# A delta-rule attention with a mixture-of-experts behind it: how the 64×64 triangular inverses are split between VectorE and TensorE

## The chip, the cores and the metric

The kernel runs on one core of one Trainium2 chip. The core has TensorE (matrix products into PSUM; PE in the profile, with PEld for its weight loads), VectorE (DVE), ScalarE (ACT), GpSimd (POOL) and SyncE (SP, which here only issues DMAs). The metric is the device time of one execution in microseconds. Each engine runs its instructions in the order in which they stand in its queue.

## The reference, cut to what matters

```python
# 4 batches x 8 heads, 768 positions, 40 features per head
for t in range(S):
    y[:, :, t] = einsum('bhd,bhde->bhe', rt, state)
    Sa = einsum('bhde,bhe->bhd', state, at)
    state_decay = state * wt - einsum('bhd,bhe->bhde', Sa, bt)
    state = state_decay + einsum('bhd,bhe->bhde', vt, kt)
# x = y as 3072 tokens of 320 features
logits = x @ w_gate;  P = exp(logits - max);  8 rounds of row and column normalisation of P
out = sum over 8 experts e of  P[:, e] * (relu(x @ w1[e]) @ w2[e])      # 320 -> 1024 -> 320
```

Everything is float32. The state of each head is updated 768 times one after the other; the kernel does this in chunks of 64 positions. Within a chunk the 64 updates depend on each other through a unit triangular 64×64 matrix I + L, so each chunk of each head needs its inverse T.

## The kernel before, in words

**Attention.** There are 12 chunks c of 64 positions, and 4 batches b; one pair (c, b) treats 8 heads, packed as NP = 4 pairs p of two heads h. Three kinds of work run at once:

- `prep` (lines 115–178) loads a chunk's inputs, forms decay products (scans `q` and `g` on VectorE, products `kb` and `ab` on GpSimd), multiplies `kb` and `ab` on TensorE (`ll`, line 159), and writes the triangular factor `lt` to a DRAM buffer `ld`. It fills one of NSX buffer sets (`sx`, `bb`, `cc`); a set is used again when the step that reads it has been done, so prep runs ahead of the recurrence by at most NSX pairs (c, b).
- The inversion, per group of two chunks (6 groups). `load_lu` reads the diagonal 32-blocks of 128 matrices back from `ld`, one block per partition. VectorE then inverts them: `inv_diag` the 8-blocks, `inv_8` from 8 to 16, `inv_16` from 16 to 32, with `contract` (lines 193 and 196: a broadcast product and a reduction). The result `un` and its transpose `tn` are written to DRAM (`finish`, lines 369–372).
- `tload` and `tmat` (lines 234–268) read the blocks back in a layout with the block's rows on partitions. For each of 16 heads-and-batches p and both heads of a pair, `tmat` merges two 32-blocks into a 64-block by two products on TensorE (`gp`, line 261; `op`, line 266), with ScalarE copies between (262, 263, 267, 268). The result stands as a block-diagonal 128×128 matrix `tt` for two heads. It is done in two halves of 8 p per chunk.
- `recur` runs the recurrence: per (c, b) the products `av`, `xc`, `pu` (line 308, the product with T), `c` and `zt`, each 4 matmuls, with evacuations on VectorE and ScalarE between. Four batches are interleaved (SKEW = 1.1).

The Python list `ev` gives each piece a time in units of a fifth of a chunk; the pieces are emitted in this order, and a planner that works with estimated durations then sets the order of each engine's queue. A float32 matmul of the program is two instructions of the TensorE queue, each with a weight load, so that the profile counts twice as many as the order does (a transposition, `zt` or `kt`, is one). In the last 20 us of attention the planner mixes in the first products of the second part.

**Mixture of experts.** Products `p` (line 582, a Strassen-like scheme with 7 products) and `op` (line 647, the second layer) run from about 485 us to the end, in an order that is mostly written out by hand. The change touches nothing of it. Its buffers use the memory that the attention's sets leave.

## Time and profile before

| | |
|---|---|
| time, median of 3 runs | 1840.1 us (1836.47 to 1844.41) |
| the profiled execution's own time | 1832.94 us |
| its span (first to last instruction) | 1831.2 us |
| TensorE busy over the span | 1724.3 us (94%) |
| VectorE / ScalarE / GpSimd busy | 1365.3 / 856.8 / 874.0 us |
| first and last `pu` product (line 308) | 117.4 and 500.7 us |
| first and last `op` product of the merge (line 266) | 114.3 and 489.7 us |

A busy time of TensorE counts each matmul from its start to its modelled end, so it overlaps and is not work at peak; the distance from one weight load to the next in a row of equal matmuls tells what one costs. In a row of the timeline, the columns are start and length of the piece in us, the engine, the line, the operation, out<-in, the shapes, and the number of instructions merged.

### The profile page before, as it was taken

How to read it: one execution, taken by the hardware profiler on the slowest of the kernel's cores; microseconds unless marked ns; L12 is line 12 of the kernel's file. 1: busy time of each engine (PE TensorE's matmuls, PEld its weight loads, DVE VectorE, ACT ScalarE, POOL GpSimd, SP SyncE). 2: the span in 40 equal slices, each digit the busy share in tenths (PEclk: the TensorE clock that was granted, in tenths of full speed). 3: DMA queues.
4: the chain of work that ended last, by engine and by line, in shares of the span. 5: the costliest groups of instructions: out<-in, count | busy, mean ns of one | idle time of the engine just before them, and what ended most of it. 6: DMA issues, size and time to landing. Idle time of an engine off the chain costs nothing.

```text
span 1831.2 us, 31655 instructions
## 1 busy us (share of the span) xinstructions
PE 1724.3 (94%) x11843; PEld 1696.8 (93%) x11843; DVE 1365.3 (75%) x2356; ACT 856.8 (47%) x1851; POOL 874.0 (48%) x854
## 2 busy tenths in 40 slices
PE   4479988999989999999999999999999999999999
PEld 4368888898978999999999999999999999999999
DVE  7786996973788867777676878977686877767675
ACT  6347767766743533434343434345343343424342
POOL 6545664723462626447291735008182644628160
PEclk8568988999999999999999999999999999999999
DMA  7468777867520101111020112201020111102001
GB/s 193 116 157 185 175 180 174 186 137 172 152 77 20 57 20 57 38 39 57 20 75 20 57 37 61 69 1 60 16 76 20 57 38 38 57 20 75 15 24 44
DMA packets 211759, 140.47 MB, mean 77 GB/s; under 512 B 162965, under 2 KB 193813, under 8 KB 211605
## 3 DMA queue, kind: packets, MB, share of 16 engines
q1 hardware_dynamic: 207925, 132.70, 27.9%
q10 hardware_dynamic: 3680, 5.74, 1.2%
q8 instruction: 94, 1.54, 0.3%
q14 instruction: 60, 0.49, 0.1%
HBM read 110.78 MB, written 27.61 MB: 76 GB/s over the span
## 4 chain that ended last, share of the span: by engine, by line
PE 75%; DVE 7%; DMA 4%; issue 4%; POOL 3%; ACT 2%; SPq 2%; POOLq 0%; ACTq 0%; DVEq 0%
PE op L647 36%; PE p L582 33%; DMA inp<-in_inp_dram 1%; PE xc L297 1%; PE av L289 1%; PE pu L308 1%; DVE pr L193 1%; DVE hl L606 1%; DVE q L124 1%; PE c L315 1%; DMA ld<-lt 1%; PE op L266 1%; DVE sm L600 1%; PE ll L159 1%; POOL ab L154 1%
## 5 line engine op out<-in xcount | busy, mean ns | idle before, releaser
L582 PE MATMUL p<-xch,wh 128*128 128x384 f32 (+1 forms) x1792 | 605.0, 339 | 8.9 <-DVE sm L600 4.3
L603 ACT ACTIVATE hh<-sm 128x384 fp32r<-128x384 f32 x512 | 269.5, 527 | 728.5 <-DVE sm L600 728.4
L647 PE MATMUL op<-wh,hh 128*128 128x320 f32 x1536 | 477.2, 311 | 4.0 <-ACT hh L603 3.8
L647 PE MATMUL op<-wl,hh 128*128 128x320 f32 x1536 | 474.8, 310 | 0.0
L647 PE MATMUL op<-wh,hl 128*128 128x320 f32 x1536 | 468.0, 309 | 0.9 <-DVE hl L606 0.9
L528 POOL TENSOR_TENSOR wl<-ws,wh 128x640 fp32r<-128x640 f32 x60 | 103.1, 1718 | 606.2 <-ACT wh L526 606.1
L606 DVE SCALAR_TENSOR_TENSOR hl<-sm,hh 128x384 fp32r<-128x384 f32 x512 | 373.1, 762 | 2.6 <-ACT hh L603 1.8
L582 PEld LDWEIGHTS p<-xch,wh 128*128 128x128 f32 (+1 forms) x1792 | 337.0, 188 | 13.3 <-DVE sm L600 5.2
L582 PE MATMUL p<-xcl,wh 128*128 128x384 f32 x896 | 302.3, 337 | 0.0
L582 PE MATMUL p<-xch,wl 128*128 128x384 f32 x896 | 301.8, 337 | 0.0
L647 PEld LDWEIGHTS op<-wh,hh 128*128 128x128 f32 x1536 | 290.2, 189 | 4.9 <-ACT hh L603 4.9
L647 PEld LDWEIGHTS op<-wl,hh 128*128 128x128 f32 x1536 | 291.1, 190 | 0.0
L647 PEld LDWEIGHTS op<-wh,hl 128*128 128x128 f32 x1536 | 286.8, 188 | 1.4 <-DVE hl L606 1.2
L600 DVE TENSOR_TENSOR sm<-p,u 128x384 f32<-128x384 f32 x384 | 236.3, 625 | 8.7
L582 PEld LDWEIGHTS p<-xcl,wh 128*128 128x128 f32 x896 | 168.6, 188 | 0.0
L582 PEld LDWEIGHTS p<-xch,wl 128*128 128x128 f32 x896 | 168.5, 188 | 0.0
L600 DVE TENSOR_TENSOR sm<-p,p 128x384 f32<-128x384 f32 x128 | 71.3, 557 | 129.4 <-PE p L582 75.0
L600 DVE TENSOR_TENSOR p<-p,p 128x384 f32<-128x384 f32 x128 | 71.1, 556 | 101.7 <-PE p L582 101.4
L600 DVE TENSOR_TENSOR u<-p,p 128x384 f32<-128x384 f32 x128 | 70.8, 553 | 57.1 <-PE p L582 55.9
L536 POOL TENSOR_TENSOR wl<-ss,wh 128x512 fp32r<-128x512 f32 x60 | 90.3, 1505 | 28.4 <-ACT wh L533 24.2
L159 PE MATMUL ll<-ab,kb 104*128 104x128 f32 x336 | 62.8, 344 | 40.5 <-POOL kb L147 18.5
L159 PEld LDWEIGHTS ll<-ab,kb 104*128 104x128 f32 x336 | 54.2, 244 | 45.3 <-POOL kb L147 24.8
(163 smaller groups left out, 2727.3 us busy)
## 6 DMA issues: line engine op xcount, KB each, us to landing
ws<-in_wts_dram SPq DMA_DIRECT2D x60, 832.0 KB, 4.5
inp<-in_inp_dram SPq DMA_DIRECT2D x42, 451.5 KB, 4.5
gd<-g SPq DMA_DIRECT2D x48, 113.8 KB, 2.6
gl<-gd SPq DMA_DIRECT2D x48, 113.8 KB, 2.8
vz<-in_v_dram SPq DMA_DIRECT2D x48, 112.0 KB, 3.5
xd<-y SPq DMA_DIRECT2D x24, 224.0 KB, 3.5
ld<-lt ACTq DMA_DIRECT2D x40, 128.0 KB, 2.6
rb<-in_r_dram SPq DMA_DIRECT2D x96, 48.0 KB, 3.1
```

The lines of the kernel that those rows point to most:

```text
L124: nc.vector.tensor_tensor_scan(out=qr.rearrange("r p t -> r (p t)"), data0=w65[:, 260:0:-1], data1=one65, initial=0.0, op0=ALU.mult, op1=A ...
L154: eng.tensor_tensor(out=ab[64:104, :, 64:128], in0=a_in[64:104], in1=g[64:104], op=ALU.mult)
L159: nc.tensor.matmul(ll[:, p], lhsT=kb[:, p], rhs=ab[:, p], start=True, stop=True)
L193: nc.vector.tensor_tensor(out=prv, in0=a.unsqueeze(2).broadcast_to([nu, n_c, n_r, n_k]), in1=m.unsqueeze(1).broadcast_to([nu, n_c, n_r, n_ ...
L266: nc.tensor.matmul(op[:, p], lhsT=gs[:, p], rhs=t2[:, p], start=True, stop=True)
L528: g.tensor_tensor(out=wl[:, 0:640], in0=raw[:, 256:896], in1=wh[:, 0:640], op=ALU.subtract)
L536: g.tensor_tensor(out=lv[:, 3:7], in0=so[:, :, 0], in1=hv[:, 3:7, 0], op=ALU.subtract)
L582: nc.tensor.matmul(o, lhsT=w_, rhs=x_, start=(j == 0), stop=(j == 3))
L600: eng.tensor_tensor(out=out, in0=x, in1=y, op=ALU.add)
L603: nc.scalar.activation(out=hh[:, f, h], in_=sm[f][:, h], func=AF.Relu)
L606: v.scalar_tensor_tensor(out=hl[:, f, h], in0=sm[f][:, h], scalar=0.0, in1=hh[:, f, h], op0=ALU.max, op1=ALU.subtract)
L647: nc.tensor.matmul(ops[i], lhsT=a[:, h, cs], rhs=w_[:, cw], start=(f == 0 and h == 0 and j == 0), stop=(last and h == 1 and j == 2))
```

## The change

VectorE now stops at blocks of 16: `inv_16`, and the copies of the off-diagonal 16-blocks that it needed (line 201 in `flip_l`, line 369 in `finish`), are taken out for all groups. TensorE does the rest. Let D be the inverse of the diagonal 16-blocks, Dᵀ its transpose, and O the part of L outside them. `tload` now loads three 64-wide tiles per chunk: `ob` (O), `dt` (Dᵀ) and `tt` (D), each with one head on partitions 0–63 and the other on 64–127. `tmat` makes four products, each of 8 p × 2 heads with 64×64 operands: `gp` = O and Dᵀ, copied to `mt`; `op` = `mt` and D, added to D in `tt`; `gq` = `mt` and the new `tt`, copied to `mq`; `oq` = `mt` and `mq`, added to `tt`. With M nilpotent of order 4 on 16-blocks, (I + M)(I + M²)D is the inverse. The copies are on ScalarE and the additions on VectorE, each over the whole 128×512 tile.

T is now stored compactly (64 columns instead of a block-diagonal 128), and `pu` is made of 8 matmuls with 64 rows instead of 4 with 128.

`ob`, `dt` and `tt` have two buffers each (`td` and `lg` had one), `tload` is emitted 1.5 units earlier relative to `tmat`, and `tmat` one unit earlier. From the third chunk on, GpSimd clears the unused quadrants of `tt`, since the sum has filled them. There are 22 buffer sets for `prep` instead of 23.

```diff
-    tt_b = [const.tile([128, 4 * NP, 128], F32, name=f"tt{i}") for i in range(NTB)]
-    td_b = [const.tile([128, 4 * NP, 32], F32, name="td")]
-    lg_b = [const.tile([128, 4 * NP, 64], F32, name="lg")]
+    tt_b, ob_b, dt_b = ([const.tile([128, 4 * NP, 64], F32, name=f"{x}{i}") for i in range(NTB)]
+                        for x in ("tt", "ob", "dt"))
+    mt_b = const.tile([128, 4 * NP, 64], F32, name="mt")
+    mq = const.tile([128, 2 * NP, 64], F32, name="mq")
...
     def flip_l(us):
...
-        nc.vector.tensor_copy(out=lu[us, 16:32, 0:16], in_=lu[us, 0:16, 16:32].rearrange("u k r -> u r k"))
...
-    def inv_16(us, i):
-        g, un_, tn_, l16 = gt(us, 16), un[us], tn[us], lu[us, 16:32, 0:16]
...
-    INV += [(inv_8, (0,)), (inv_8, (1,)), (flip_h, ()), (inv_16, (0,)), (inv_16, (1,)), (inv_16, (2,))]
+    INV += [(inv_8, (0,)), (inv_8, (1,)), (flip_h, ())]
 
     def tload(c):
...
+        w = 16
+        if c >= NTB:
+            for h in range(0, 128, 64):
+                nc.gpsimd.memset(tt[h:h + 32, :, 32:64], 0.0)
         for h in range(2):
-            nc.sync.dma_start(out=lb[q[h], :, q[h]],
-                              in_=ld[cc, 0:32].rearrange("j b p h s -> j (b p) h s")[:, :, h, 32:64])
-        for h in range(2):
-            nc.sync.dma_start(out=t1[q[h]], in_=nd[u[0][h]].rearrange("g j s -> j g s"))
-        for h in range(2):
-            nc.sync.dma_start(out=t2[q[h]], in_=ud[u[1][h]].rearrange("g j s -> j g s"))
+            for a in range(0, 64 - w, w):
+                nc.sync.dma_start(out=ob[h * 64 + a:h * 64 + a + w, :, a + w:64],
+                                  in_=ld[cc, a:a + w].rearrange("j b p h s -> j (b p) h s")[:, :, h, a + w:64])
+        for blk in range(2):
+            for h in range(2):
+                q, r = slice(blk * 32, blk * 32 + 32), slice(h * 64 + blk * 32, h * 64 + blk * 32 + 32)
+                nc.sync.dma_start(out=dt[r, :, q], in_=nd[u[blk][h]].rearrange("g j s -> j g s"))
         for h in range(2):
             for blk in range(2):
-                r = slice(h * 64 + blk * 32, h * 64 + blk * 32 + 32)
-                nc.sync.dma_start(out=tt[r, :, r], in_=ud[u[blk][h]].rearrange("g j s -> j g s"))
+                q, r = slice(blk * 32, blk * 32 + 32), slice(h * 64 + blk * 32, h * 64 + blk * 32 + 32)
+                nc.sync.dma_start(out=tt[r, :, q], in_=ud[u[blk][h]].rearrange("g j s -> j g s"))
 
+    def tprod(name, lhs, rhs):
+        o = pt.tile([128, 2 * NP, 64], F32, name=name, tag="pt")
+        for p in range(2 * NP):
+            for h in range(0, 128, 64):
+                nc.tensor.matmul(o[h:h + 64, p], lhsT=lhs[h:h + 64, p], rhs=rhs[h:h + 64, p], start=True, stop=True)
+        return o
+
     def tmat(c, half):
         gl = slice(half * 8, half * 8 + 8)
...
-        gp = pt.tile([64, 2 * NP, 32], F32, name="gp", tag="pt")
-        for p in range(2 * NP):
-            nc.tensor.matmul(gp[:, p], lhsT=lb[:, p], rhs=t1[:, p], start=True, stop=True)
-        nc.scalar.copy(out=gs[0:32, :, 0:32], in_=gp[0:32])
-        nc.scalar.copy(out=gs[32:64, :, 32:64], in_=gp[32:64])
-        op = pt.tile([64, 2 * NP, 32], F32, name="op", tag="pt")
-        for p in range(2 * NP):
-            nc.tensor.matmul(op[:, p], lhsT=gs[:, p], rhs=t2[:, p], start=True, stop=True)
-        nc.scalar.copy(out=tt[0:32, :, 32:64], in_=op[0:32])
-        nc.scalar.copy(out=tt[64:96, :, 96:128], in_=op[32:64])
+        ob, dt, tt = (x[:, gl] for x in tts[c])
+        mt = mt_b[:, gl]
+        gp = tprod("gp", ob, dt)
+        nc.scalar.copy(out=mt, in_=gp)
+        op = tprod("op", mt, tt)
+        nc.vector.tensor_tensor(out=tt, in0=op, in1=tt, op=ALU.add)
+        gp = tprod("gq", mt, tt)
+        nc.scalar.copy(out=mq, in_=gp)
+        op = tprod("oq", mt, mq)
+        nc.vector.tensor_tensor(out=tt, in0=op, in1=tt, op=ALU.add)
...
         for p in range(NP):
-            nc.tensor.matmul(pu[:, p], lhsT=tts[c][:, b * NP + p], rhs=x1[:, p], start=True, stop=True)
+            for h in range(0, 128, 64):
+                nc.tensor.matmul(pu[h:h + 64, p], lhsT=tts[c][2][h:h + 64, b * NP + p], rhs=x1[h:h + 64, p],
+                                 start=True, stop=True)
...
-        nc.vector.tensor_copy(out=tn[us, 16:32, 0:16], in_=un[us, 0:16, 16:32].rearrange("u c j -> u j c"))
...
-        t = 5 * c + 2 - T_LEAD
+        t = 5 * c + 2 - T_LEAD - 1
...
-NSX = 23
+NSX = 22
...
-L_LEAD = 0.5
+L_LEAD = 2
```

The planner moves the work of the queues around these products. On TensorE, at the place where the first chunk's T is made and the first step of the recurrence takes it (`ll` and `kt` are products of `prep`, `xc` and `av` of the recurrence), there stood before:

```order
L167 MATMUL kt<-cst,kb 128x104 x4
L261 MATMUL gp<-td,lg 64x32 x8
L266 MATMUL op<-td,lg 64x32 x8
L261 MATMUL gp<-td,lg 64x32 x8
L308 MATMUL pu<-x_966,tt_217 128x104 x4
L297 MATMUL xc_1030<-f,sx_214 104x104 x4
```

and now:

```order
L250 MATMUL gp<-dt_215,ob_213 64x64 x15
L161 MATMUL ll<-ab_219,kb 128x128 x4
L169 MATMUL kt<-cst,kb 128x104 x4
L250 MATMUL gp<-dt_215,ob_213 64x64
L250 MATMUL op<-tt_211,mt 64x64 x16
L161 MATMUL ll<-ab_220,kb 128x128 x4
L169 MATMUL kt<-cst,kb 128x104 x4
L250 MATMUL gq<-tt_211,mt 64x64 x16
L161 MATMUL ll<-ab_219,kb 128x128 x4
L169 MATMUL kt<-cst,kb 128x104 x4
L250 MATMUL oq<-mq,mt 64x64 x16
L250 MATMUL gp<-dt_215,ob_213 64x64 x16
```

(then `ll` once, and `pu` of the first step). Between the four products stand those of three more pairs of `prep`, which before came after the first `pu`; there are 17 pairs of `ll` and `kt` ahead of the first `pu` instead of 14. The products of 64×64 form 72 separate runs in TensorE's queue before and 130 after, `pu` counted with them after.

On VectorE, after the copy that follows the 16-blocks of the first group, there stood before:

```order
L207 COPY tn<-un 128x2x8x8
L193 TENSOR_TENSOR pr<-un,lu 128x1024
L128 RECIPROCAL g_223<-q 112x4
L169 TENSOR_TENSOR st_188<-ll,cst 64x8x64
L196 TENSOR_REDUCE gt<-pr 128x8x8
L134 SCALAR_TENSOR_TENSOR g<-inp,g_223 112x260
L193 TENSOR_TENSOR pr<-un,lu 128x1024
```

and so on to the twelfth piece of `inv_16`, and now:

```order
L208 COPY tn<-un 128x2x8x8
L130 RECIPROCAL g_221<-q 112x4
L136 SCALAR_TENSOR_TENSOR g<-inp,g_221 112x260
L171 TENSOR_TENSOR st_179<-ll,cst 64x8x64
L126 SCALAR_TENSOR_TENSOR q<-inp,cst 112x260
```

What is left there is work of `prep`.

On TensorE, where the first products of the experts (`p`) stand among those of the recurrence, there stood before, with three steps (`pu`) of the recurrence still to come:

```order
L261 MATMUL gp<-td,lg 64x32
L582 MATMUL p_5735<-xch_5628,wh_5630 128x384
L582 MATMUL p_5735<-xcl_5629,wh_5630 128x384
L289 MATMUL av<-rb_231,vz_225 104x128 x4
L582 MATMUL p_5735<-xch_5628,wl_5631 128x384
```

and now, with eight steps still to come:

```order
L250 MATMUL gq<-tt_211,mt 64x64 x16
L333 MATMUL zt<-cst,z 40x104 x4
L313 MATMUL c_6338<-pm,bb_185 104x104 x4
L579 MATMUL p_7109<-xch_7002,wh_7004 128x384
L579 MATMUL p_7109<-xcl_7003,wh_7004 128x384
L579 MATMUL p_7109<-xch_7002,wl_7005 128x384
```

Eight of these products stand there together, and the next ones only after six more steps of the recurrence.

More of the change, by code (lines that the diff above doesn't have):

```diff
@@ L73, in attention @@
     luf = inv.tile([128, 1056], F32, name="lu")
-    prf = inv.tile([128, 1024], F32, name="pr")
-    gtf = inv.tile([128, 256], F32, name="gt")
+    prf = inv.tile([128, 512], F32, name="pr")
+    gtf = inv.tile([128, 64], F32, name="gt")
     tnf = inv.tile([128, 1056], F32, name="tn")
@@ L90, in clear @@
         nc.gpsimd.memset(tnf, 0.0)
-        for t in vz_b + rb_b + c1_b + lg_b:
+        for t in vz_b + rb_b + c1_b:
             nc.vector.memset(t, 0.0)
@@ L94, in clear @@
             nc.gpsimd.memset(t[96:RL], 0.0)
-        for t in tt_b:
-            nc.gpsimd.memset(t, 0.0)
+        for ts in zip(dt_b, ob_b, tt_b):
+            for t in ts:
+                nc.gpsimd.memset(t, 0.0)
     fresh = set(range(NSX))
@@ L104, in first_use @@
                            in_=cst[64:R2, 360:400].unsqueeze(1).broadcast_to([40, 8, 40]))
-    state = {"sx": 0, "ab": 0, "g1": 0, "vz": 0, "c1": 0, "t1": 0, "tt": 0, "rb": 0, "y": 0}
+    state = {"sx": 0, "ab": 0, "g1": 0, "vz": 0, "c1": 0, "t1": 0, "tt": 0, "ob": 0, "dt": 0, "rb": 0, "y": 0}
     def rot(key, lst):
@@ L238, in tload @@
         cc = GRP[c][1]
-        q = [slice(h * 32, h * 32 + 32) for h in range(2)]
         u = [[slice(cc * 64 + blk * 32 + h * 16, cc * 64 + blk * 32 + h * 16 + 16) for h in range(2)]
              for blk in range(2)]
+        w = 16
+        if c >= NTB:
+            for h in range(0, 128, 64):
+                nc.gpsimd.memset(tt[h:h + 32, :, 32:64], 0.0)
         for h in range(2):
-            nc.sync.dma_start(out=lb[q[h], :, q[h]],
-                              in_=ld[cc, 0:32].rearrange("j b p h s -> j (b p) h s")[:, :, h, 32:64])
```

17 lines of the change are left out of this document (2 added, 15 removed).

## The prediction

> **What bounds the kernel now.** I read the busy times by stretch first, then the rows of the stretch that the change touches. Columns: stretch, length, busy time and count of PE, PEld, DVE, ACT, POOL, then PE's granted clock, DMA share and GB/s.
>
> ```profile
> 0.00:117.00 117.00, 57.92 (x294) 51.55 (x294) 86.73 (x157) 56.32 (x140) 68.04 (x98) 0.63 0.66 159
> 117.00:500.00 383.00, 353.29 (x3337) 338.50 (x3337) 285.03 (x495) 264.76 (x656) 194.64 (x229) 0.93 0.75 170
> 500.00:600.00 100.00, 88.05 (x522) 83.16 (x521) 84.01 (x161) 40.37 (x79) 41.47 (x38) 0.97 0.14 44
> 600.00:1831.00 1231.00, 1225.02 (x7697) 1223.59 (x7695) 909.56 (x1545) 495.33 (x976) 569.81 (x491) 1.00 0.13 43
> ```
>
> From 600 us the experts keep TensorE full, and the change does not touch them. It acts in two stages. Up to 117 us TensorE is half idle: the first T is not there. From 117 to 500 us, the 48 steps of the recurrence, TensorE is busy 92% at a mean clock of 0.93, VectorE 74%. So work taken from VectorE there buys little by itself, and work given to TensorE costs nearly its full length. The chain that ended last says the same of the whole:
>
> ```profile
> PE 75%; DVE 7%; DMA 4%; issue 4%; POOL 3%; ACT 2%; SPq 2%; POOLq 0%; ACTq 0%; DVEq 0%
> ```
>
> **Change, part 1: what leaves VectorE.** The 128x1024 products and their sums are `inv_16`'s alone; with the last copy in `finish` (min/median/max ns):
>
> ```profile
> L193 DVE TENSOR_TENSOR pr<-gt,tn 128x1024 f32<-128x1024 f32 x18 | 22.6, 1257 | 0.0
> L193 DVE TENSOR_TENSOR pr<-un,lu 128x1024 f32<-128x1024 f32 x18 | 22.1, 1229 | 0.0
> L196 DVE TENSOR_REDUCE gt<-pr 128x64 f32<-128x1024 f32 x12 | 14.5, 1205 | 0.1
> L196 DVE TENSOR_REDUCE un<-pr 128x64 f32<-128x1024 f32 x12 | 14.4, 1203 | 0.0
> L196 DVE TENSOR_REDUCE gt<-pr 128x128 f32<-128x1024 f32 x6 | 7.2, 1204 | 0.0
> L196 DVE TENSOR_REDUCE un<-pr 128x128 f32<-128x1024 f32 x6 | 7.2, 1202 | 0.0
> L369 DVE COPY tn<-un x6: 348/369/567, 101.0 to 417.2; 128x256 f32<-128x256 f32 x6
> L290 DVE TENSOR_TENSOR f<-av,cst 104x512 f32<-104x512 f32 x48 | 32.6, 680 | 29.1 <-PE av L289 28.9
> ```
>
> That is 88.0 + 2.3 us, and as much again for the copy in `flip_l`: 92 us. Back come 48 additions of 128x512 from PSUM, nearest to the `f` row: 48 × 0.68 = 33. VectorE gains 60 us, most of it before 417 us. ScalarE's 96 copies of 0.36 become 48 of about 0.6: no change that counts.
>
> **Part 2: what TensorE gets.** The price of a matmul instruction is the distance of weight loads in a row of them. At full clock:
>
> ```profile
> L261 PEld LDWEIGHTS gp<-td,lg x384: 129/135/228, 110.4 to 484.0; 64*64 64x64 f32 x192
> L308 PEld LDWEIGHTS pu<-x,tt x384: 186/192/337, 117.4 to 500.7; 128*128 128x128 f32 x192
> L297 PEld LDWEIGHTS xc<-f,sx x512: 166/172/297, 19.4 to 496.8; 104*104 104x104 f32 x171
> 357.98 1.00 PEld L261 LDWEIGHTS gp<-td,lg 64*64 64x64 f32 x16 [1.76 <-issue]
> 355.02 0.97 PEld L308 LDWEIGHTS pu<-x,tt 128*128 128x128 f32 x8
> 360.29 1.54 PEld L297 LDWEIGHTS xc<-f,sx 104*104 104x104 f32 x16
> ```
>
> A 64x64 instruction costs (1.00 − 0.135)/15 = 58 ns, one of `pu` (0.97 − 0.192)/7 = 111 ns, one of `xc` (104 columns stream) (1.54 − 0.172)/15 = 91 ns. Before, TensorE gives 768 × 0.058 = 44.5 us to the merge and 384 × 0.111 = 42.6 to `pu`. After, it has 24 halves × 4 products × 16 matmuls × 2 = 3072 instructions in the merges and 768 in `pu`, alternating in pairs between the upper and the lower partitions. All hangs on whether two such halves overlap. The trace has one place where the last `op` (partitions 64–127) met the first `gp` (0–63), at half clock:
>
> ```profile
> 114.25 1.46 PEld L266 LDWEIGHTS op<-td,lg 64*64 64x64 f32 x13 [2.08 <-ACT lg L263]
> 115.56 0.18 PEld L261 LDWEIGHTS gp<-td,lg 64*64 64x64 f32 x1
> 115.60 0.22 PEld L266 LDWEIGHTS op<-td,lg 64*64 64x64 f32 x1
> 115.62 0.22 PEld L261 LDWEIGHTS gp<-td,lg 64*64 64x64 f32 x1
> 115.70 0.22 PEld L266 LDWEIGHTS op<-td,lg 64*64 64x64 f32 x1
> 115.73 0.22 PEld L261 LDWEIGHTS gp<-td,lg 64*64 64x64 f32 x1
> 115.81 0.22 PEld L266 LDWEIGHTS op<-td,lg 64*64 64x64 f32 x1
> ```
>
> Alone, `op` loads come every (1.46 − 0.22)/12 = 0.10 us; in the mixed stretch still every 0.10 to 0.11, and a `gp` load sits in each gap. Two for the price of one. I take this for full clock too: 29 ns per 64x64 instruction, 3072 × 0.029 = 89 us; for `pu`, whose streamed side is `xc`'s, 91/2: 768 × 0.0455 = 35. The bounds are this and no overlap (58 and 91 ns).
>
> A third term is the change of form. A row of 64x64 products between full ones:
>
> ```profile
> 347.53 0.30 PEld L308 LDWEIGHTS pu<-x,tt 128*128 128x128 f32 x2
> 347.94 1.00 PEld L266 LDWEIGHTS op<-td,lg 64*64 64x64 f32 x16
> 348.98 0.30 PEld L308 LDWEIGHTS pu<-x,tt 128*128 128x128 f32 x2
> ```
>
> The second `pu` load began at 347.64, so the next was due at 347.75 and came at 347.94; the last `op` load began at 348.81, the next was due at 348.87 and came at 348.98. In and out cost 0.19 + 0.11 = 0.30 us. The order has 72 such runs before, 130 after: 22 us against 39.
>
> Sum: before 44.5 + 42.6 + 22 = 109; after 89 + 35 + 39 = 163. TensorE gets 54 us more, and at the stage's clock of 0.93, 58 us.
>
> **Part 3: the front.** The first T came when group 0's inversion had gone through DRAM:
>
> ```profile
> 77.36 1.22 DVE L193 TENSOR_TENSOR pr<-un,lu 128x1024 f32<-128x1024 f32 x1
> 101.04 0.57 DVE L369 COPY tn<-un 128x256 f32<-128x256 f32 x1
> 106.92 2.06 PE L159 MATMUL ll<-ab,kb 104*128 104x128 f32 x8 [1.40 <-POOL kb L147]
> 110.40 1.91 PE L261 MATMUL gp<-td,lg 64*64 64x32 f32 x16 [0.73 <-DMA td<-nd]
> 117.41 2.03 PE L308 MATMUL pu<-x,tt 128*128 128x104 f32 x8
> PE ll L159 <- POOL kb L147: 17.7, 6, 4.7
> 359.03 0.97 PEld L159 LDWEIGHTS ll<-ab,kb 104*128 104x128 f32 x8
> 359.91 0.43 PEld L167 LDWEIGHTS kt<-cst,kb 104*128 104x128 f32 x4
> ```
>
> Twelve pieces of 1.2 us leave this chain: 14.6 us, so `gp` could start near 95. But the merge is longer (four products of 1.7 us at half clock and four evacuations of 0.6 to 0.7, about 11 us for the first half, against 7), and `ll` of the fourteenth pair, at 106.9, stands ahead of `gp`, with three more pairs between the four products. These come at GpSimd's pace, 6 to 7 us apart here, perhaps 4.5 without `inv_16` between their scans. So the first `pu` stays near 117 (112 to 122). What is won is that three pairs of `prep` are done by then: 3 × (0.97 + 0.43) = 4 us less for TensorE later.
>
> **Part 4: waits given back.** From 117 to 500 us TensorE is idle 29.7 us, from 500 to 600 us 12. With VectorE 60 us lighter I give back a third of the first, 10 us; four dependent products with an evacuation behind each bring new waits, so not more. Before 600 us the experts' products stand earlier among the recurrence's, but only eight of them: half of the 12, 6 us.
>
> **DMA.** Each chunk issues 14 loads instead of 10, 48 more in all, each about half a microsecond of SP:
>
> ```profile
> 108.83 2.08 SPq L252 DMA_DIRECT2D tt<-ud x4
> ```
>
> 25 us more on SP. The loads of O can go before the inversion is done, the others are emitted 2.5 units ahead of where they were, with a second buffer: I price it at nothing. What is queued behind them are `inp`, `gl`, `rb`; if these become late, see the rivals. One set less lets `prep` run ahead one pair less; nothing in the waits shows a set being late. GpSimd's 20 small clears of `tt` fall on an engine that is half idle there.
>
> Total: 58 − 4 − 10 − 6 = +38 on the profiled execution's 1832.9 us: 1871. The median of the runs lies 7 us higher, the sum stands halfway between the two: **1874 us**.
>
> **Rivals.** *The halves don't overlap at full clock.* No row shows more than two loads and two multiplications begun in 107 ns (the mixed stretch). I read this as the array at half clock; it could be the rate at which TensorE takes instructions. Then a pair costs 107 ns at any clock: 3840 × 0.0535 = 205, with 39 for the runs 244 instead of 163, +87 in all: 1961. It decides from about 45 ns per instruction. For it: the mixed stretch is cold, and the only one; against: the same clock halves the single rate as well.
>
> The Trainium skill (TensorE: Matmul & The Clock Gate, section "Wait — 56ns, not 53.3ns?") says that starts of matmuls never come closer than about 25 ns. Counted for multiplications alone this would leave the first sum standing; an estimate that counts weight loads too gives 100 ns for a pair, this rival.
>
> *VectorE's release decides: faster.* If the waits were mostly VectorE's lateness, TensorE would get back all its idle time (29.7 + 12), a clock of 1.0 instead of 0.93 (27 us of the 383), and 10 us at the front. That is 79, against 54 + 0: 1808 as the end; with two thirds of it, 1834. For it: in 0 to 117 us the clock is 0.63, which shows what idling costs, and VectorE ran 85% from 200 to 300 us:
>
> ```profile
> 200.00:300.00 100.00, 90.75 (x871) 86.93 (x869) 85.16 (x141) 71.87 (x183) 61.43 (x68) 0.93 0.81 180
> 400.00:500.00 100.00, 95.85 (x932) 92.31 (x933) 55.43 (x97) 68.22 (x160) 38.98 (x46) 0.95 0.68 163
> ```
>
> Against: from 400 to 500 us, with hardly any inversion left, TensorE is no less full. It decides when more than 54 us come back.
>
> *SP or the chain of four products paces the steps.* Half of SP's added 25 us exposed, or 0.5 us of wait at each of the 96 products with nothing of part 4 given back: some +25, 1899.
>
> **Numbers.** Forecast 0.45 (own range 1850 to 1900), no overlap 0.24, VectorE's release 0.21, pacing 0.10. What a measurement of this kernel can tell from no change is about 0.5%, 9 us: faster 0.21, same 0.10, slower 0.69. The range, 1826 to 1962, takes in the better half of the second and nearly all of the first and fourth cases.
>
> **What would show it.** Right: merge loads 29 ns apart on average at full clock; TensorE above 92% in the stage of the steps, its end 30 to 45 us later; VectorE near 65%. Wrong: loads 50 to 58 ns apart (no overlap), or steps at 8 us each as now, (500 − 117)/48, with VectorE idle (release). A first `pu` before 110 us would refute part 3.

## The result, and the profile after

| | before | after |
|---|---|---|
| time, median of 4 runs | 1838.7 us (1836.5 to 1844.4) | 1907.3 us (1905.2 to 1909.1) |
| the profiled execution's own time | 1832.9 us | 1906.5 us |
| its span | 1831.2 us | 1904.6 us |
| mean granted clock of TensorE | 0.959 | 0.957 |
| first and last `pu` product | 117.4 and 500.7 us | 113.0 and 573.3 us |

The changed kernel is slower: the ratio is 1.038, with a 95% interval of 1.036 to 1.040. That is 69 us more, where the forecast was some 35 more. The page of the kernel after, its busy times and the shares of the chain that ended last:

```profile
PE 1786.7 (94%) x14531; PEld 1741.7 (91%) x14531; DVE 1307.4 (69%) x2319; ACT 848.7 (45%) x1802; POOL 842.3 (44%) x877
...
PE 78%; DVE 7%; DMA 7%; issue 3%; SPq 2%; POOL 2%; ACT 1%; ACTq 0%; DVEq 0%; POOLq 0%
```

VectorE has lost 58 us of its 1365.3, TensorE has gained 62, and the share of DMA in the chain has gone from 4% to 7%. Where the time lies is read from the busy times by stretch, cut at each kernel's own first and last `pu` (columns as in the prediction). First the kernel before, then the kernel after:

```profile
0.00:117.40 117.40, 58.33 (x296) 51.89 (x296) 87.11 (x158) 56.32 (x140) 68.04 (x98) 0.63 0.66 159
117.40:500.70 383.30, 353.59 (x3340) 338.87 (x3339) 285.16 (x496) 264.76 (x656) 194.91 (x229) 0.93 0.75 169
500.70:1831.20 1330.50, 1312.36 (x8211) 1306.05 (x8209) 993.08 (x1704) 535.70 (x1055) 611.01 (x527) 1.00 0.13 43
```

```profile
0.00:113.00 113.00, 60.85 (x398) 54.12 (x398) 67.76 (x136) 53.95 (x133) 63.16 (x102) 0.65 0.70 171
113.00:573.30 460.30, 410.94 (x5924) 378.42 (x5925) 250.28 (x481) 259.04 (x614) 168.74 (x248) 0.93 0.61 142
573.30:1904.60 1331.30, 1314.88 (x8214) 1309.19 (x8209) 989.39 (x1704) 535.72 (x1055) 610.38 (x527) 0.99 0.13 43
```

The 73 us of span are split in this way: the front is 4.4 us shorter, the stage of the 48 steps is 77.0 longer (460.3 against 383.3), and what follows is 0.8 longer. Of the 77.0, TensorE's busy time takes 57.4 (410.9 − 353.6) and its idle time 19.6 (49.4 − 29.7). The first of these is what the prediction asked for (58). The second has the opposite sign of what it asked for (−10).

### The profile page after: what moved, and what is told of

The parts are those of the page before. It is cut to its first block, busy times and chain, and to the rows that moved or that the text cites. A ratio compares the mean times of both kernels' runs of the same rounds, so it can differ in the third digit from the quotient of the medians.

```text
span 1904.6 us, 37021 instructions
## 1 busy us (share of the span) xinstructions
PE 1786.7 (94%) x14531; PEld 1741.7 (91%) x14531; DVE 1307.4 (69%) x2319; ACT 848.7 (45%) x1802; POOL 842.3 (44%) x877
## 4 chain that ended last, share of the span: by engine, by line
PE 78%; DVE 7%; DMA 7%; issue 3%; SPq 2%; POOL 2%; ACT 1%; ACTq 0%; DVEq 0%; POOLq 0%
PE op L644 35%; PE p L579 32%; DMA inp<-in_inp_dram 3%; PE xc L293 2%; PE c L313 1%; DMA rb<-in_r_dram 1%; PE av L285 1%; PE pu L305 1%; DMA ld<-lt 1%; DVE q L126 1%; PE gp L250 1%; PE ll L161 1%; PE op L250 1%; PE gq L250 1%; PE oq L250 1%
## 5 line engine op out<-in xcount | busy, mean ns | idle before, releaser
L533 POOL TENSOR_TENSOR wl<-ss,wh 128x512 fp32r<-128x512 f32 x60 | 91.0, 1517 | 32.5 <-ACT wh L530 28.2
L708 DVE SCALAR_TENSOR_TENSOR acc<-op,pmat,acc 128x320 f32<-128x320 f32 x168 | 91.2, 543 | 4.6 <-PE op L644 4.5
L126 DVE TENSOR_TENSOR_SCAN q<-inp,cst 112x260 f32<-112x260 f32 x42 | 29.3, 698 | 92.7 <-DMA inp<-in_inp_dram 72.4
```

The source lines that it names most:

```text
L126: nc.vector.tensor_tensor_scan(out=qr.rearrange("r p t -> r (p t)"), data0=w65[:, 260:0:-1], data1=one65, initial=0.0, op0=ALU.mult, op1=A ...
L533: g.tensor_tensor(out=lv[:, 3:7], in0=so[:, :, 0], in1=hv[:, 3:7, 0], op=ALU.subtract)
L708: nc.vector.scalar_tensor_tensor(out=acc[:, m], in0=ops[i], scalar=pmat[:, n, e:e + 1], in1=acc[:, m], op0=ALU.mult, op1=ALU.add)
```

## Do the two halves overlap?

The price of the added products hung on this. A stretch of the timeline of the kernel after, TensorE's weight loads at full clock (1.00 granted from 402 to 408 us):

```profile
403.21 0.92 PEld L285 LDWEIGHTS av<-rb,vz 104*104 104x104 f32 x8
404.27 1.01 PEld L250 LDWEIGHTS gq<-tt,mt 64*64 64x64 f32 x32
405.35 0.30 PEld L333 LDWEIGHTS zt<-cst,z 104*40 104x40 f32 x4
405.63 0.81 PEld L313 LDWEIGHTS c<-pm,bb 128*104 128x104 f32 x8
406.55 0.73 PEld L305 LDWEIGHTS pu<-x,tt 64*64 64x64 f32 x16
407.41 0.44 PEld L293 LDWEIGHTS xc<-f,sx 104*104 104x104 f32 x4
L250 PEld LDWEIGHTS gq<-tt,mt x768: 129/135/228, 96.8 to 558.9; 64*64 64x64 f32 x192
L305 PEld LDWEIGHTS pu<-x,tt x768: 129/133/228, 113.0 to 573.3; 64*64 64x64 f32 x192
```

A run of 32 takes (1.01 − 0.135)/31 = 28.2 ns per instruction: two instructions of 64×64 in the time of one (58). `pu` takes (0.73 − 0.133)/15 = 39.8 ns; 45.5 had been priced. The halves overlap at full clock, and the rival "no overlap" is out. These are means: in the run of `gq`, the loads of the two halves begin 7 ns apart, and the next pair about 50 ns later.

The price of a change of form is in the same rows. A load of `av` takes about 0.18 us, so its last one begins at 403.95 and `gq` 0.32 us later; the last load of `gq` begins at 405.15 and `zt` 0.20 later. With 0.11 and 0.03 us as the usual distances, going in costs 0.21 and coming out 0.17. That is about 0.4 us for a run, and the same for `pu` between `c` and `xc` (0.30 was priced). The trace has 130 runs, as the order has. Since 28.2 and 39.8 lie under the priced 29 and 45.5, the sum comes out a little higher only: 87 + 31 + 130 × 0.4 = 170 against 163.

## Where the idle time shows: late loads

In the kernel after, `inp`, the input of `prep`, comes late more often. These are the waits of the stage for it, before and after (waiting engine and line, what it waited for, us in total, times, longest):

```profile
DVE q L124 <- DMA inp<-in_inp_dram: 17.5, 9, 5.6
```

```profile
DVE q L126 <- DMA inp<-in_inp_dram: 56.0, 13, 8.8
```

One such wait as the timeline of the kernel after shows it, SP's queue (SPq) with it:

```profile
296.60 2.25 SPq L235 DMA_DIRECT2D ob<-ld  x3
298.89 0.60 SPq L240 DMA_DIRECT2D dt<-nd  x1
...
303.11 1.65 SPq L240 DMA_DIRECT2D dt<-nd  x3
304.80 0.57 SPq L269 DMA_DIRECT2D vz<-in_v_dram  x1
305.47 0.74 SPq L120 DMA_DIRECT2D inp<-in_inp_dram  x1
306.25 0.57 SPq L269 DMA_DIRECT2D vz<-in_v_dram  x1
306.93 0.56 SPq L120 DMA_DIRECT2D inp<-in_inp_dram  x1
...
310.88 0.70 DVE L126 TENSOR_TENSOR_SCAN q<-inp,cst 112x260 f32<-112x260 f32 x1 [8.81 <-DMA inp<-in_inp_dram]
311.55 0.58 DVE L308 TENSOR_TENSOR pm<-pu,cst 128x416 f32<-128x416 f32 x1
...
312.28 0.85 PE L333 MATMUL zt<-cst,z 104*40 104x104 f32 x4 [6.68 <-DVE g L130]
```

Three loads of `dt`, 1.65 us of SP, stand ahead of `inp`, and four more loads of T, 2.85 us, a little before them. VectorE sits 8.8 us in front of the scan `q`. Behind the scan in its queue stands `pm`, which belongs to the recurrence and has nothing to do with `inp`. TensorE stands still for 6.7 us before `zt`, until VectorE's `g`, which follows the scan. So a late load for `prep` stops a step. Whether the load is late because of what stands ahead of it is what the experiment with the loads on another queue asks.

The stage has two halves: the one while `prep` still runs (up to the last `ll`), and the rest. Before, with 28 steps begun in the first and 20 in the second:

```profile
117.40:367.90 250.50, 225.81 (x2088) 216.61 (x2088) 206.37 (x352) 176.81 (x446) 149.67 (x174) 0.91 0.78 176
367.90:500.70 132.80, 127.79 (x1254) 122.25 (x1252) 78.79 (x144) 87.95 (x210) 45.24 (x55) 0.96 0.67 156
```

After, with 26 and 22:

```profile
113.00:399.30 286.30, 249.94 (x3466) 229.79 (x3467) 162.38 (x326) 169.45 (x411) 118.17 (x181) 0.92 0.68 157
399.30:573.30 174.00, 161.00 (x2461) 148.63 (x2460) 87.89 (x156) 89.59 (x203) 50.57 (x67) 0.94 0.50 117
```

TensorE's idle time goes from 24.7 to 36.4 us in the first half and from 5.0 to 13.0 in the second. A step takes 8.9 us and then 11.0 in the first half, 6.6 and then 7.9 in the second.

## Experiments

For each kernel the median is set against the median of the kernel before on the same chip, so "+55" is 55 us over that. The changed kernel stands at +69. Stage means first to last `pu`. The rows are of one execution each. The planner orders the queues anew for each kernel, so a run shows its edit together with what the new order moved.

### 1. VectorE's release alone

The kernel before, without `inv_16` and its two copies. This leaves the off-diagonal 16-blocks out of T, so part of the work is not done by anybody.

```diff
-        nc.vector.tensor_copy(out=lu[us, 16:32, 0:16], in_=lu[us, 0:16, 16:32].rearrange("u k r -> u r k"))
-    INV += [(inv_8, (0,)), (inv_8, (1,)), (flip_h, ()), (inv_16, (0,)), (inv_16, (1,)), (inv_16, (2,))]
+    INV += [(inv_8, (0,)), (inv_8, (1,)), (flip_h, ())]
-        nc.vector.tensor_copy(out=tn[us, 16:32, 0:16], in_=un[us, 0:16, 16:32].rearrange("u c j -> u j c"))
```

> The kernel before with the 16-to-32 step of the inversion left out (inv_16 and the two copies that serve it), so T lacks the off-diagonal 16-blocks; the merge on TensorE, the loads and the 23 sets stay. It gives VectorE's release alone. Theory 1 (the steps are paced by TensorE's own queue): TensorE's 353.6 busy us in the stage of the steps stay, only part of its 29.7 idle us and some of the front come back: 10 to 25 us less than before. Theory 2 (VectorE's lateness paces the steps): the stage gets shorter by about the 92 us taken out or a good part of it: 50 us less or more.

Measured: 1833.6 us, ratio 0.997 (0.995 to 0.999), −5 us. The stage of this kernel:

```profile
99.90:493.20 393.30, 359.72 (x3360) 342.47 (x3360) 219.92 (x448) 269.45 (x668) 169.25 (x235) 0.93 0.74 169
```

VectorE has 65 us less to do there than before (219.9 against 285.2), and the first `pu` comes 17.5 us earlier. The stage is nonetheless 10 us longer, and TensorE idles 33.6 us in it instead of 29.7. Part of this is work that moved: 16 pairs of `prep` have their `ll` ahead of the first `pu`, 18 in the kernel before, so two more fall into the stage. What the change takes off VectorE was worth 5 us; neither theory had it so small. The rival "VectorE's release decides" is out by the direct measurement.

### 2. The overlap taken away

The kernel after, with all products of the upper partitions first and then those of the lower ones:

```diff
-        for p in range(2 * NP):
-            for h in range(0, 128, 64):
+        for h in range(0, 128, 64):
+            for p in range(2 * NP):
```

> The changed kernel with the two loops in each merge product swapped: all 8 products of the upper partitions, then all 8 of the lower, so that neighbours in the queue are on the same half and hardly overlap. Theory 1: 3072 instructions go from 28 ns to nearly 58 ns apiece, with some overlap where the two rows of 16 meet: 60 to 90 us more than the changed kernel. Theory of late loads and chain waits as the pace (TensorE's own length does not matter any more): under 25 us more.

Measured: 1947.6 us, ratio 1.059 (1.055 to 1.063), +109, so 40 more than the changed kernel. Its stage, and a run of the merge at full clock:

```profile
107.90:614.80 506.90, 488.90 (x5940) 458.26 (x5939) 254.92 (x490) 260.79 (x617) 171.86 (x250) 0.92 0.57 131
456.31 1.76 PEld L250 LDWEIGHTS oq<-mq,mt 64*64 64x64 f32 x32
```

(1.76 − 0.135)/31 = 52.4 ns per instruction. The mean takes in the few loads in the middle where the two halves meet and overlap; the others are 58 to 59 ns apart. So without neighbours of the other half, the overlap is gone. TensorE's busy time grows by 78 us against the changed kernel, as 3072 × 24 ns = 74 ask. The time grows by only 40, because the idle time falls from 49.4 to 18.0 and the first `pu` comes 5 us earlier. With more to do, TensorE has less to wait for. Both expectations missed: 60 to 90 us, if TensorE's length set the time, was too much, and under 25, if it did not matter, too little. A little more than half of the added length was paid.

### 3. Only two of the four products

The kernel after without `gq`, `oq`, the copy to `mq` and the second addition. T then lacks the terms of second and third order in M.

```diff
-        gp = tprod("gq", mt, tt)
-        nc.scalar.copy(out=mq, in_=gp)
-        op = tprod("oq", mt, mq)
-        nc.vector.tensor_tensor(out=tt, in0=op, in1=tt, op=ALU.add)
```

> The changed kernel without its third and fourth product (gq, oq, their copy and addition left out), so T lacks the terms of second and third order. Theory 1 (TensorE's length in the stage sets the time): 1536 instructions x 28.3 ns = 43 us less, the number of runs of 64x64 products stays (126 against 130), and some waits go with the shorter chain: 43 to 60 us less than the changed kernel. Theory of late loads as the pace: the loads are all still there, so under 20 us less.

Measured: 1855.3 us, ratio 1.010 (1.006 to 1.014), +20, so 49 less than the changed kernel, within the 43 to 60 that TensorE's length asked for. The stage gives 37 of it (423.1 against 460.3) and the front 15, where the first `pu` comes at 97.8 us instead of 113.0. In its stage TensorE is busy 35 us less than in the changed kernel's. The whole stage, then its part after the last `ll`:

```profile
97.80:520.90 423.10, 375.48 (x4477) 341.73 (x4474) 241.76 (x478) 251.00 (x601) 182.88 (x257) 0.92 0.69 158
364.60:520.90 156.30, 143.47 (x1816) 130.47 (x1816) 76.00 (x148) 84.17 (x193) 50.13 (x67) 0.95 0.60 134
```

With two products the merge's instructions cost 1536 × 28.2 ns = 43 us, no more than the 44.5 of the kernel before; those of `pu` cost 31 instead of 42.6, and VectorE has no `inv_16`. Still the kernel is 1% slower than the one before. It has 126 runs of the narrow form instead of 72. At the prices read above that is 126 × 0.4 = 50 us instead of 22, which takes more than the 13 that merge and `pu` save; this part is worked out and not measured alone. TensorE's idle time in the stage is 47.6 us, nearly that of the changed kernel, and 12.8 in the second half, where the changed kernel has 13.0. So most of the excess of idle time doesn't need the chain of four products: it is there with two.

### 4. T's loads taken off SP

The kernel after, with all 14 loads of `tload` issued by ScalarE:

```diff
-                nc.sync.dma_start(out=ob[h * 64 + a:h * 64 + a + w, :, a + w:64],
+                nc.scalar.dma_start(out=ob[h * 64 + a:h * 64 + a + w, :, a + w:64],
...
-                nc.sync.dma_start(out=dt[r, :, q], in_=nd[u[blk][h]].rearrange("g j s -> j g s"))
+                nc.scalar.dma_start(out=dt[r, :, q], in_=nd[u[blk][h]].rearrange("g j s -> j g s"))
...
-                nc.sync.dma_start(out=tt[r, :, q], in_=ud[u[blk][h]].rearrange("g j s -> j g s"))
+                nc.scalar.dma_start(out=tt[r, :, q], in_=ud[u[blk][h]].rearrange("g j s -> j g s"))
```

> The changed kernel with the 14 loads of T per chunk issued from ScalarE's queue instead of SP's. Theory A (the input loads of prep come late because SP issues the many loads of T ahead of them, and block VectorE and GpSimd): VectorE's wait for inp shrinks from 72 us to under 30 and the time falls by 5 to 15 us. Theory B (SP's queue is not what makes inp late): the time stays within 5 us or grows by what ScalarE loses to 168 issues of about 0.5 us.

Measured: 1893.6 us, ratio 1.029 (1.027 to 1.031), +55, so 14 less than the changed kernel; the intervals are apart. The halves of its stage (26 and 22 steps), and the wait for `inp`:

```profile
120.20:384.50 264.30, 239.91 (x3439) 220.63 (x3440) 152.94 (x304) 164.53 (x398) 113.58 (x173) 0.95 0.72 165
384.50:558.40 173.90, 162.41 (x2463) 150.08 (x2463) 86.43 (x158) 89.28 (x203) 49.97 (x67) 0.94 0.50 117
DVE q L126 <- DMA inp<-in_inp_dram: 41.0, 11, 5.9
```

The stage is 22 us shorter than the changed kernel's, all of it in the first half, with as many steps (264.3 against 286.3); the second half is the same to 0.1. Of the 22, 12 are idle time: 24.4 us in the first half, what it was before the change. The other 10 are busy time at a higher granted clock, with the same work (239.9 × 0.95 and 249.9 × 0.92, 228 and 230 us at full clock). The waits for `inp` fall from 56 to 41 us, over the whole kernel from 72 to 51, where theory A expected under 30: the time came out as it expected, the wait only in part. The first `pu` comes 7 us later than in the changed kernel, which takes a third of the gain away; 19.5 pairs of `prep` are begun by then instead of 17.25, so a part of the stage's work has moved ahead of it. In this kernel, having the loads on SP costs 14 us in all, where they were priced at nothing.

The Trainium skill (DMA: Bandwidth & Descriptors, section "Issuing engines are not separate DMA queues") says that issuing from several engines only saves the sequencer's time, which is usually small beside the transfer. For single loads the trace agrees: SP takes 1.65 us for three loads of `dt`, and an `inp` lands 4.6 us after its issue in the median. Over the 168 loads of `tload` it was not small in this run, 14 us; experiments 5 and 7, with the same edit in other kernels, have 6 and 3 us.

### 5. The same edit on the kernel before

All ten loads of `tload` by ScalarE in the kernel before:

```diff
-            nc.sync.dma_start(out=lb[q[h], :, q[h]],
+            nc.scalar.dma_start(out=lb[q[h], :, q[h]],
...
-                nc.sync.dma_start(out=tt[r, :, r], in_=ud[u[blk][h]].rearrange("g j s -> j g s"))
+                nc.scalar.dma_start(out=tt[r, :, r], in_=ud[u[blk][h]].rearrange("g j s -> j g s"))
```

> The kernel before with the 10 loads of T per chunk issued from ScalarE's queue. Tells whether the 14 us that the same edit gave the changed kernel belong to its larger and earlier loads. If late loads behind SP are a cost of the changed kernel alone: within 5 us of the kernel before. If they are a cost of both: 8 to 14 us less.

Measured: 1829.9 us, ratio 0.996 (0.993 to 0.999), −6, between the two expectations. The stage is 1.5 us shorter, and its waits for `inp` fall from 17.5 us:

```profile
117.10:498.90 381.80, 360.81 (x3345) 342.95 (x3344) 289.18 (x500) 266.62 (x661) 193.82 (x228) 0.92 0.75 170
DVE q L124 <- DMA inp<-in_inp_dram: 10.0, 8, 3.1
```

Before the change the loads on SP cost less than half as much time. But TensorE's idle time in the stage falls here too, from 29.7 to 21.0 us, against 49.4 to 35.9 in experiment 4. Of the idle time that goes with loads on SP, the greater part was there before the change. With the loads on ScalarE in both kernels, the change costs 61 us (+55 against −6) instead of 69. By the intervals of the three ratios, what SP adds to the cost of the change lies between about 1 and 15 us. This kernel is also a little faster than both, the one before and the one after.

### 6. GpSimd's product taken out of the recurrence

Of TensorE's waits in the stage of the kernel after, those before `zt` are the largest group: four, 18.2 us together. One is the 6.7 us shown above; another ended with GpSimd's `z` (a row of its timeline):

```profile
441.23 0.88 PE L333 MATMUL zt<-cst,z 104*40 104x104 f32 x4 [5.51 <-POOL z L328]
```

The kernel after, with `z` of all chunks on VectorE (in both kernels this is so from the tenth chunk on):

```diff
-        (nc.vector if c >= 9 else nc.gpsimd).tensor_tensor(out=z, in0=ws[:, :, 64:104],
+        nc.vector.tensor_tensor(out=z, in0=ws[:, :, 64:104],
```

> The changed kernel with z of all chunks on VectorE (before: GpSimd for chunks 0 to 8). Theory A (the new idle time of TensorE comes from z standing behind work of GpSimd that waits for late loads): the idle time before zt, 18 us, loses the share in which GpSimd released it, 5 to 11 us less. Theory B (it comes from the chain of four dependent products): no change within 4 us. Theory C (z is late because pm on VectorE is late): no change or a few us more, since VectorE gets 0.33 us per step more.

Measured: 1902.8 us, ratio 1.035 (1.033 to 1.037), +64. Set against 1.036 to 1.040 for the changed kernel, this is hardly to be told from no change. The idle time before `zt` fell from 18.2 to 5.1 us, that before `gq` rose from 5.2 to 16.3. Most of what was taken away at one place came up at another.

### 7. Both edits together

The kernel after with the edits of experiments 4 and 6.

```diff
-                nc.sync.dma_start(out=ob[h * 64 + a:h * 64 + a + w, :, a + w:64],
+                nc.scalar.dma_start(out=ob[h * 64 + a:h * 64 + a + w, :, a + w:64],
...
-        (nc.vector if c >= 9 else nc.gpsimd).tensor_tensor(out=z, in0=ws[:, :, 64:104],
+        nc.vector.tensor_tensor(out=z, in0=ws[:, :, 64:104],
```

> The changed kernel with both edits that took waits away: the loads of T from ScalarE's queue, and z on VectorE. If the waits behind late loads are what they have in common and they add up: 14 + 4, so about 1889 us; TensorE's idle time in the stage falls from 49 to about 30 us, that of the kernel before, and what is left over it is TensorE's longer work, 57 us. If they remove the same wait: 1893 us as with the loads alone.

Measured: 1901.0 us, ratio 1.037 (1.034 to 1.040), +66. A miss for both expectations: the 14 us of experiment 4 are all but gone again. The stage of this kernel, then its first half:

```profile
121.10:570.30 449.20, 410.63 (x5899) 378.65 (x5899) 251.98 (x495) 253.20 (x601) 148.91 (x204) 0.93 0.62 142
121.10:391.70 270.60, 245.21 (x3439) 226.09 (x3440) 163.69 (x329) 164.18 (x398) 102.90 (x148) 0.93 0.71 161
```

The idle time is 38.6 us, 11 less than in the changed kernel, and 25.4 in the first half, so this part of experiment 4 is there again. But the granted clock is 0.93 as in the changed kernel, not 0.95, so the busy time is the changed kernel's, and the first `pu` comes 8 us later. What 4 shows firmly is the idle time in the first half, 12 us; its lower busy time hung on a clock that was not there with the other edit. Gains of this size don't add up.

### 8. `pu` in halves on the kernel before

The kernel before, `pu` made of eight products of 64 rows that take the diagonal blocks of `tt`:

```diff
-            nc.tensor.matmul(pu[:, p], lhsT=tts[c][:, b * NP + p], rhs=x1[:, p], start=True, stop=True)
+            for h in range(0, 128, 64):
+                nc.tensor.matmul(pu[h:h + 64, p], lhsT=tts[c][h:h + 64, b * NP + p, h:h + 64], rhs=x1[h:h + 64, p],
+                                 start=True, stop=True)
```

> The kernel before with pu alone changed to 8 matmuls of 64 rows (each head's 64x64 block of T). TensorE: 384 x 0.111 = 42.6 us become 768 x 0.040 = 30.5, but the order has 107 separate runs of 64x64 products instead of 72, 35 x 0.33 = 11.6 us. Theory 1: the two cancel, within 5 us of the kernel before. If changes of form cost nothing in the end: 10 us less. If the halves of pu do not overlap: 768 x 0.09 = 69, 35 us more.

Measured: 1839.1 us, ratio 1.003 (1.000 to 1.005). The halves save 384 × 111 − 768 × 39.8 ns = 12 us of `pu` and pay about 0.4 us for each of 35 more runs of the narrow form (107 in the trace instead of 72), 14. The two nearly cancel, as expected; the result, some 4 us more, is hardly to be told from nothing.

### 9. The overlap on the kernel before

The kernel before, with `op` of the first half of a chunk alternating with `gp` of the second, so that a chunk has three steps instead of four and the middle one overlaps:

```diff
+            if op is not None:
+                nc.tensor.matmul(op[:, p], lhsT=gs0[:, p], rhs=t2[:, p], start=True, stop=True)
+            if gp is not None:
+                nc.tensor.matmul(gp[:, p], lhsT=lb[:, p], rhs=t1[:, p], start=True, stop=True)
...
-        for half in range(2):
-            ev.append((t + 2 * SKEW * half, tmat, (c, half)))
+        for k in range(3):
+            ev.append((t + SKEW * k, tmat, (c, k)))
```

> The kernel before with the op products of the first half of a chunk (partitions 64 to 127) set alternately with the gp products of the second half (0 to 63). Inversion, loads and sets are unchanged. Theory 1: 12 chunks x 16 instructions x 0.058 = 11 us of TensorE's time overlap, 5 more runs cost 1.6: 5 to 12 us less than before. If TensorE's length did not set the time, within 4 us.

Measured: 1845.6 us, ratio 1.005 (1.003 to 1.007), +10, where 5 to 12 us less, or a change within 4, was expected. Its stage:

```profile
114.90:513.00 398.10, 362.65 (x3336) 345.56 (x3337) 282.95 (x495) 264.78 (x656) 194.72 (x229) 0.88 0.73 163
```

Busy time by the granted clock, as an estimate, gives 362.65 × 0.88 = 319 us of work at full clock, against 353.59 × 0.93 = 329 before. So some 10 us of work are saved. But the granted clock is lower, the idle time is 35.5 us instead of 29.7, and the stage is longer. Taking work from TensorE did not shorten it.

### 10. The merge in full form

The question was now whether TensorE's work bounds the stage at all when it is made less. The kernel before, with the merge as block-diagonal 128×128 products for two p at a time, one run of `gp` and one of `op` for a chunk, in the same form as everything around them. Half of its 16 loads are on ScalarE, and it has 22 sets:

```diff
-    lg_b = [const.tile([128, 4 * NP, 64], F32, name="lg")]
+    lg_b = [const.tile([128, 2 * NP, 128], F32, name=x) for x in ("lb", "gs")]
...
-        gp = pt.tile([64, 2 * NP, 32], F32, name="gp", tag="pt")
+        gp = pt.tile([128, 2 * NP, 32], F32, name="gp", tag="pt")
...
-            nc.tensor.matmul(gp[:, p], lhsT=lb[:, p], rhs=t1[:, p], start=True, stop=True)
+            nc.tensor.matmul(gp[:, p], lhsT=lb[:, p], rhs=t1_t[:, p], start=True, stop=True)
...
-        for half in range(2):
-            ev.append((t + 2 * SKEW * half, tmat, (c, half)))
+        ev.append((t, tmat, (c,)))
```

> The kernel before with its merge in the full 128x128 form: two p (one on partitions 0 to 63, one on 64 to 127) in one block-diagonal product, the whole chunk at once, 8 matmuls for gp and 8 for op; 8 of its 16 loads per chunk go from ScalarE's queue, and 22 sets make room. TensorE: 384 instructions x 0.111 = 43 us instead of 768 x 0.058 = 44.5, and none of the 72 changes of form (22 us). Theory 1 with the price of the form right: 15 to 25 us less than before, with 5 of it perhaps from the loads on ScalarE. If changes of form cost nothing in the end (other waits take their place): within 6 us of the kernel before.

Measured: 1856.9 us, ratio 1.012 (1.010 to 1.014), +21, a miss in sign. The halves of its stage (27 and 21 steps):

```profile
122.70:374.10 251.40, 211.77 (x1832) 205.81 (x1833) 201.94 (x336) 174.04 (x437) 142.32 (x167) 0.91 0.75 173
374.10:507.90 133.80, 122.97 (x1115) 121.33 (x1113) 80.85 (x137) 85.94 (x209) 37.96 (x47) 0.92 0.63 144
```

TensorE's busy time falls by 18.9 us (334.7 against 353.6), near what was worked out (1.5 and 22 at full clock), and its idle time rises by 20.7. The first half is as long as before the change (251.4 against 250.5) with 14 us less busy time in it. The edit does more than take work away: it has 16 loads for a chunk instead of 10, and it merges a chunk at once, so that its first step waits for all of it. This run doesn't tell these apart from the form.

### 11. One set less

The kernel before with 22 buffer sets, as the changed kernel has:

```diff
-NSX = 23
+NSX = 22
```

> The kernel before with 22 sets for prep instead of 23, nothing else. Theory (sets are not short): within 5 us of the kernel before. If one set less makes prep late: 10 us or more added, and a part of what the changed kernel lost.

Measured: 1831.8 us, ratio 0.998 (0.997 to 1.000). The missing set costs nothing in the kernel before, so it is an unlikely cause of the change's result and of that of experiment 10. (23 sets in the changed kernel were not tried.)

### 12. Both engines relieved at once

Experiment 10 with the omission of experiment 1 (T again lacks the off-diagonal 16-blocks). If TensorE and VectorE bound the stage together, taking from both should pay where taking from one does not.

```diff
-    INV += [(inv_8, (0,)), (inv_8, (1,)), (flip_h, ()), (inv_16, (0,)), (inv_16, (1,)), (inv_16, (2,))]
+    INV += [(inv_8, (0,)), (inv_8, (1,)), (flip_h, ())]
```

> The run e9 (merge in the full form, without changes of form) with the 16-to-32 step left out as in e1 (T lacks the off-diagonal 16-blocks). Each edit alone left the stage of the steps as long as it was, 385 and 393 us against 383. Theory D (TensorE's length and VectorE's work bind together in the kernel before, so that either alone turns into idle time): the stage falls to about 365 us, 25 us or more less than e9, so 1825 or below. Theory E (the floor of the stage is neither of the two but the chain of a step with its loads and the order of the queues): within 12 us of e9 less the 5 us that e1 gave, 1840 to 1857.

Measured: 1829.7 us, ratio 0.996 (0.993 to 0.999), −8. The halves of its stage (27 and 21 steps):

```profile
98.50:350.20 251.70, 214.18 (x1827) 209.63 (x1826) 155.88 (x316) 176.11 (x442) 128.52 (x179) 0.88 0.79 179
350.20:485.70 135.50, 124.28 (x1154) 122.53 (x1153) 62.68 (x120) 90.00 (x219) 35.32 (x45) 0.95 0.64 143
```

The first half takes 251.7 us, where it took 251.4 with 46 us more on VectorE and 250.5 with 51 and 12 us more on VectorE and TensorE. What was gained against experiment 10 was gained ahead of the stage: the first `pu` came at 98.5 us instead of 122.7. Two pairs of `prep` more fall into this first half (16 instead of 18 lie ahead of the first `pu`), so it is not quite the same work in the same time. The time lies between the two expectations, 1825 or below and 1840 to 1857. The stage, 387.2 us, is not the 365 that the theory of two joint bounds asked for: relieving both did not shorten it. What does set the 250 us stays open. In the rows the DMA share (0.75 to 0.79) and what moved (173 to 179 GB/s) are alike in all three kernels, and no run here was made to change the bytes. The order of the queues is another candidate, and so is the granted clock, 0.88 here and 0.91 in the other two.

## Why the prediction was right, and where it was wrong

The time, 1907 us, is slower as forecast and lies within the stated range of 1826 to 1962. But that range was drawn to take in most of four cases. The measured time is 7 us outside the forecast's own range (1850 to 1900), and the price nearest to it is that of a rival, pacing, at 1899. What was right is the sign and TensorE's added work, not the total.

**TensorE's added work: right in sum.** TensorE's busy time in the stage rose by 57.4 us; 58 was predicted. By an estimate with the two-digit clocks of the rows, the work at full clock rose by 410.94 × 0.93 − 353.59 × 0.93 = 53.3 against 54. The terms under it were each off: merge 87 us (89 priced), `pu` 31 (35), changes of form some 52 (39). With 109 before, these would ask for 170 − 109 = 61, so the sum is closer than its terms, and that part is luck. The decision for the overlap, from a few half-clock loads, holds at full clock.

The rule of the Trainium skill that the prediction weighed (TensorE: Matmul & The Clock Gate, section "Wait — 56ns, not 53.3ns?", starts of matmuls not below about 25 ns) does not hold start by start in this trace. In the run of `gq` shown above, the multiplications of the two halves begin 6 or 7 ns apart and the next pair about 52 ns later; only their mean, 28.2 ns, is above 25, and the measurement decides. The estimate that counted weight loads too, 100 ns for a pair, is out: a pair with its loads takes 56.

**The front (part 3): right in time, wrong in a detail.** The first `pu` came at 113.0 (112 to 122 predicted). But the three pairs of `prep` that were to be won by then were not: in the trace 18 pairs had begun their `ll` before the first `pu` before the change, and not 14, and 17 and a bit after. The −4 us written for them came about as a first `pu` 4.4 us earlier, not as less work later. That the number fits is luck.

**Waits given back (part 4): this is the step that failed.** The prediction gave back 10 us of TensorE's idle time in the stage because VectorE became lighter, and 6 us behind it. Measured: 19.6 us more idle time in the stage, and a length behind it that is 0.8 us more, where busy and idle time are the same within 2.6 us. The two misses make 36 us, and the forecast's own sum of +38 on the span missed the 73 by 35. Experiment 1 speaks against the credit: with VectorE's release alone TensorE idles 33.6 us in the stage instead of 29.7, and the kernel gains 5 us. That VectorE was at 85% for 100 us showed a busy engine, not one that something waited for at the end.

**DMA priced at nothing: wrong, by some 8 us.** The prediction named what is queued behind the loads of T (`inp` first of all) and then put no price on it. Moving the 14 loads of a chunk off SP takes 14 us back and brings the idle time of the first half from 36.4 to 24.4. But the kernel before gains from this too. With the loads on ScalarE in both kernels, the change costs 61 us instead of 69, and TensorE's idle time in the stage grows by 14.9 us (35.9 against 21.0) instead of 19.6. So of the 20 us of added idle time about 5 are shown to come with the loads on SP. For the other 15 no run found the owner. Experiment 3 shows that the chain of four products is not needed for nearly as much idle time, and experiment 2, with all loads on SP and 18.0 us, that the idle time is no fixed sum.

**VectorE's release decides: refuted**, by experiment 1 (−5 us, where the rival needed more than 54 and priced up to 79). **No overlap: refuted**, by the load distances; in experiment 2, where the merge has lost most of it, TensorE is busy 78 us more and the kernel 40 us slower. **SP or the chain paces the steps:** it was given as a rival in the place of the forecast, at +25. This price fits its first term alone: half of SP's 25 us is 12.5, or 28 with the 16 us of part 4 not given back; 0.5 us at 96 products is 48, or 64. It also comes out slower, so that the chance of "slower" should have been 0.79, not 0.69. What came was in addition to the forecast's sum: SP's share is about 8 us, and with half of the chain gone (experiment 3) the stage idles nearly as long.

**What would show it.** Merge loads 29 ns apart: 28.2. VectorE near 65%: in the stage 250.3/460.3 = 54%, 69% over the span. TensorE above 92% in the stage: it was 89%, and this row was the one to show that part 4 was wrong. The last `pu` 30 to 45 us later: it came 73 later.

**A premise that holds in part.** The prediction said that work taken from VectorE buys little, and experiment 1 bears it out: some 90 us taken, 5 gained. It said that work given to TensorE costs nearly its length. For the change itself this holds: the 57.4 us of busy time are in the stage in full. In experiment 2 it does not: 78 us more of busy time made the stage 47 us longer and the kernel 40. It also read TensorE's 92% as a bound, and a bound would pay back what is taken off it. Experiments 9 and 10 took some 10 and 19 us off TensorE in the stage and the stage did not get shorter, though both edits moved other work too.

## What to carry to other kernels

Cost added work on the fullest engine from the distance of its instructions in a row, and add the price of each change of the tiles' form; here that sum came out within 1 us, in part by luck. Don't credit waits as given back unless a row shows that the relieved engine is what ended them: the credit of 16 us and the 20 us of new idle time made half of the result. Price what is queued behind added loads on the queue that issues them, and try the same cure on the kernel before, or the cure's whole gain will be put down to the change. In this kernel, where several engines are nearly balanced, added work was paid for by half to its full length, and removed work returned next to nothing.

## What the runs showed of the hardware that was not expected

- Float32 products of 64×64 on the upper and lower 64 partitions, in turn, cost 28.2 ns per instruction at full clock, half of the 58 of a row that stays on one side, and with 104 streamed columns 39.8 ns, where half the full-size product's streaming gave 45.5. With all of one side first it is 52.4, and 58 to 59 away from the place where the sides meet.
- A run of 64×64 products among larger ones cost about 0.4 us of TensorE for going in and out, in a run of 16 instructions and in one of 32; the trace has 130 runs, of 2 to 64 instructions, in the kernel after.
- The granted clock of the same stage was between 0.88 (experiment 9) and 0.95 (experiment 4), in kernels whose stages hold different work of TensorE. But with the same work, 382 us by an estimate from busy time times clock, it was 0.93 in experiment 7 and 0.95 in experiment 4. For 350 us of work that is, as an estimate, 350/0.88 − 350/0.95 = 29 us, as much as most effects here. A part of it is not the kernel's: over the whole span, 25 executions of the kernel before on one chip had 0.948 to 0.960. What sets it was not settled.
